# The first batch of an attention and MLP kernel, loaded with seven consecutive tokens to a partition

## The chip, the cores and the metric

The kernel runs on one core of a Trainium2 chip. The metric is the device time of one execution in microseconds, as a median of several runs. Its engines are named as in the profile: PE multiplies matrices (PEld loads its weights), DVE, ACT and POOL work on vectors, SP issues transfers. Each engine takes its instructions in order, and waits on semaphores for the others.

## The reference

`q`, `k`, `v` are (8, 12, 448, 64): 8 batches, 12 heads, 448 tokens, 64 dimensions, float32.

```python
def rmsnorm(x, g):
    rms = np.sqrt(np.mean(x * x, axis=-1, keepdims=True) + 1e-06)
    return x / rms * g
q_n, k_n = (rmsnorm(q, g_q), rmsnorm(k, g_k))
scores = np.matmul(q_n, k_n.transpose(0, 1, 3, 2)) / np.sqrt(64)
attn = softmax(scores)
x = np.matmul(attn, v)          # then heads side by side: (8, 448, 768)
xn = (x - mean(x)) / np.sqrt(var(x) + 1e-06) * g_ln
out = x + np.maximum(xn @ w_ch1, 0.0) @ w_ch2      # 768 -> 3072 -> 768
```

## The kernel before

**Tiling.** Heads go in pairs (48 of them, six to a batch). A pair has seven *groups* of 128 rows by 64 columns for each of q, k, v: for either head three groups with tokens 3p, 3p+1, 3p+2 on partition p (tokens 0 to 383, "main", `load_main`, L128), and one group with the last 64 tokens of both heads, one head on either half of the partitions ("left", `load_left`, L136). One or two pairs make a *unit*; batch 0 is units 0 to 3 (one, one, two, two pairs), later batches have three units each.

**Preparing a unit** (`pieces`, L190). The letters are those of the order below: `a`, `c` square k and q on ACT (L216); `d`, `e` sum the squares on DVE (L219); `g` takes the roots on ACT (L222, L223: logarithm, exponential), for unit 0 apart as `gq` and `gk`; `i` multiplies k by the product of the two gains, "kg" (L230, on DVE for units 0 and 1, else POOL; the product itself is L228); `j` casts that to a 16-bit high half (POOL L236, ACT L238 in unit 0) and `k` makes the low half from the difference (DVE L241); `l` scales q by its root (DVE L68); `m` duplicates it (L280, on POOL for units 1, 2 and 4); `z` casts the values to 16 bits (POOL L286, L292). The key is not scaled by its root: the exponential of the scores takes it as its scale, one number to each partition.

**Attention of a pair.** `K` (`trans_k`, L309) and `Q` (`trans_q`, L321) turn the groups over on PE into one row of PSUM, and copy that to `kU` and `qU` (DVE L319, ACT L334 or DVE L336). `S p.i` (`scores`, L340) multiplies group i of the keys with all queries of the head (L354; the left group L364, L365) and takes the exponential on ACT (L372). `V p.i` multiplies these with the values (L409, L411), which end as a tile of tokens by 128 columns of `x` (L424 to L431). `T` takes statistics for the layer norm. From unit 8 on, transfers on SP's queue turn k and q over in place of PE (L259 to L272).

**The order.** Batch 0 stands in an order written out by hand, `ORDER`: every engine has its instructions in that order. Its beginning:

```python
b0 a0 c0 L4 i0 j0 e0 k0 gq0 l0 b1 m0 a1 c1 K0 Q0 d0 G gk0 S0.0 S0.1 d1 e1 L5 i1 g1 j1 l1 k1 m1
z0 b2 a2 S0.2 d2 c2 S0.3 S0.4 K1 V0.0 e2 i2 S0.5 Q1 g2 l2 S0.6 S1.0 j2 V0.1 S1.1 S1.2 m2 b3
```

`L4`, `L5` load the units of batch 1. From batch 1 on, pieces of the attention of the next batch are dealt out between the chunks of the MLP of the one before (L653 up, L669 down).

**The first loads** (`load_first`, L138). They go into memory that the MLP uses later (`hT`, `w2`). SP begins with the main part of q of pair 0 and its two left halves, ACT with the same of k; POOL loads the two gains (L151) and the left part of k of pairs 1 to 5; all else follows on SP: k of pair 1 main, q left of pairs 1 to 5, then pair by pair.

**Stores** (`store`, L705): an x tile of 128 tokens goes out in one transfer of 128 rows, the left tokens in two of 64 rows.

Of the kernel before, what the change touches and what calls it, by code (L numbers as in the profile page):

```python
# [8 lines left out]
FP32 = mybir.dt.float32  # L9
# [7 lines left out]
ts = bass.ts  # L17

B, H, S, D = 8, 12, 448, 64
DM, FF = 768, 3072  # L20
NDC, NFF = DM // 128, FF // 128
NPAIR = H // 2
# [4 lines left out]
EXP_BIAS = -4.0  # L27
# [6 lines left out]


ORDER = """
b0 a0 c0 L4 i0 j0 e0 k0 gq0 l0 b1 m0 a1 c1 K0 Q0 d0 G gk0 S0.0 S0.1 d1 e1 L5 i1 g1 j1 l1 k1 m1
z0 b2 a2 S0.2 d2 c2 S0.3 S0.4 K1 V0.0 e2 i2 S0.5 Q1 g2 l2 S0.6 S1.0 j2 V0.1 S1.1 S1.2 m2 b3
V0.2 a3 V0.3 k2 c3 S1.3 K2 V0.4 S1.4 z2 V0.5 Q2 S1.5 V0.6 V1.0 i3 W0 d3 e3 S1.6 V1.1 V1.2 S2.0
j3 T0 V1.3 S2.1 S2.2 Q3 V1.4 S2.3 K3 S2.4 V1.5 V1.6 S2.5 g3 z3 S2.6 V2.0 S3.0 S3.1 V2.1 k3  # L40
S3.2 b4 S3.3 V2.2 l3 a4 V2.3 m3 S3.4 V2.4 K4 S3.5 Q4 V2.5 V2.6 S3.6 Q5 S4.0 V3.0 S4.1 V3.1 i4
V3.2 d4 T1 K5 V3.3 W1 c4 V3.4 V3.5 S4.2 S4.3 V3.6 S4.4 S4.5 W2 e4 V4.0 V4.1 j4 S4.6 S5.0 k4
S5.1 g4 V4.2 l4 S5.2 V4.3 V4.4 V4.5 S5.3 K6 V4.6 z4 V5.0 S5.4 m4 b5 V5.1 G2 S5.5 L6 V5.2 S5.6
# [33 lines left out]
class _Fast:  # L77
# [53 lines left out]
    def load_left(self, eng, n, t, b, h0, nh):  # L131
# [3 lines left out]
        for e in range(2):  # L135
            eng.dma_start(t[64 * e:64 * e + 64], left[e])  # L136

    def load_first(self):  # L138
        nc = self.nc
        flat = self.hT.rearrange("p f n -> p (f n)").bitcast(FP32)  # L140
        t = [flat[:, 2688 * n:2688 * n + 2688].rearrange("p (w g d) -> p w g d", w=NPAIR, d=D)
             for n in range(2)]
        flat = self.sh.w2.rearrange("p f n -> p (f n)").bitcast(FP32)
        t.append(flat[:, 128:128 + 2688].rearrange("p (w g d) -> p w g d", w=NPAIR, d=D))
        main = lambda eng, n, p: self.load_main(eng, n, t[n][:, p, 0:6], 0, 2 * p, 2)
        left = lambda eng, n, p=0, m=NPAIR: self.load_left(eng, n, t[n][:, p:p + m, 6], 0, 2 * p, 2 * m)
        for n, eng in ((0, nc.sync), (1, nc.scalar)):
            main(eng, n, 0)
            left(eng, n, 0, 1)
        for n in range(2):  # L150
            nc.gpsimd.dma_start(self.sh.gg[:, n], self.gs[n].unsqueeze(0).broadcast_to([128, D]))  # L151
        left(nc.gpsimd, 1, 1, NPAIR - 1)
        main(nc.sync, 1, 1)
        left(nc.sync, 0, 1, NPAIR - 1)
        for n, p in ((0, 1), (1, 2), (1, 3), (0, 2), (0, 3), (2, 0), (2, 1)):
            main(nc.sync, n, p)
        left(nc.sync, 2)
        for n, p in ((1, 4), (1, 5), (0, 4), (0, 5)):
            main(nc.sync, n, p)
        for p in range(2, NPAIR):  # L160
            main(nc.sync, 2, p)
        self.v_first = t[2]
        for u, (b, hs, m) in enumerate(UNITS):
            if b == 0:
                self.loads[u] = [x[:, hs // 2:hs // 2 + m].rearrange("p w g d -> p (w g) d")
                                 for x in t]

    def load_unit(self, u):
        nc = self.nc
        b, hs, m = UNITS[u]  # L170
        t = self.p_in.tile([128, 3, 14, D], FP32, tag="qkv", name="qkv")
        eng = self.nc.sync if u < 11 else self.nc.gpsimd
        for n in (1, 0, 2):
            self.load_main(nc.gpsimd if u == 10 and n == 2 else eng, n, t[:, n, 0:6 * m], b, hs, 2 * m)
            self.load_left(eng, n, t[:, n, 6 * m:7 * m], b, hs, 2 * m)
        self.loads[u] = [t[:, n] for n in range(3)]

# [12 lines left out]
    def pieces(self, u):  # L190
# [9 lines left out]
        def begin():  # L200
            c["t"] = self.loads.pop(u)
            c["ssq"] = self.p_n.tile([128, 2, 14], FP32, tag="ssq", name="ssq")[:, :, 0:g]
            c["rt"] = self.p_n.tile([128, 2, 14], FP32, tag="rt", name="rt")[:, :, 0:g]
            c["rb"] = self.p_n.tile([128, 2, 14], FP32, tag="rq", name="rr_all", bufs=6)[:, :, 0:g]
            c["r", 0], c["r", 1] = c["rb"][:, 0], c["rb"][:, 1]
            c["qn"] = self.p_n.tile([128, 14, 2, D], FP16, tag="qn", name="qn")[:, 0:g]
            c["khl"] = self.p_n.tile([128, 14, 2, D], FP16, tag="khl", name="khl")[:, 0:g]
            self.units[u] = (c["qn"], c["khl"], m, c["r", 1])

        def square(n):  # L210

# [6 lines left out]
        def total(n):  # L218
            nc.vector.tensor_reduce(out=c["ssq"][:, n], in_=c["sq", n], axis=AX.X, op=ALU.add)  # L219

        def root(n=slice(0, 2)):
            nc.scalar.activation(c["rt"][:, n], c["ssq"][:, n], AFT.Ln, bias=D * 1e-6)  # L222
            nc.scalar.activation(c["rb"][:, n], c["rt"][:, n], AFT.Exp, scale=-0.5)  # L223


        def kg():
            if u == 0:
# [53 lines left out]
                                                            in_=c["qn"][:, :, 0])  # L281

        def vmain():
            o = v16.rearrange("p s h j d -> p (s h) j d") if UNITS[u][0] else v16.rearrange(
                "p s h j d -> p s (h j) d")
            nc.gpsimd.tensor_copy(out=o[:, :, :, 0:D], in_=c["t"][2][:, 0:6 * m].rearrange(  # L286
                "p (h j) d -> p h j d", j=3) if UNITS[u][0] else self.v_first[:, p0:p1, 0:6])

        def vleft():
            for e in range(2):  # L290
                r = slice(64 * e, 64 * e + 64)
                nc.gpsimd.tensor_copy(  # L292
                    out=vl[r, :, e, 0:D],
                    in_=c["t"][2][r, 6 * m:] if UNITS[u][0] else self.v_first[r, p0:p1, 6])

        def vall():

# [3 lines left out]
            vleft()  # L301

        return dict(b=begin, a=lambda: square(1), c=lambda: square(0), d=lambda: total(1),
                    e=lambda: total(0), gq=lambda: root(0), gk=lambda: root(1), g=root, i=kg,
                    j=khi, k=klo, l=qn, m=qdup, v=vmain, w=vleft, x=dma_k, y=dma_q,
                    z=vall if u == 0 else lambda: (vmain(), vleft()))

# [1 line left out]
    def trans_k(self, p):  # L309
        nc, sh = self.nc, self.sh  # L310
        u, w = PAIR_UNIT[p]
        qn, khl = self.units[u][0:2]
        kT, ps = self.kU[PE_SET][:, 960 * (p % 2):960 * (p % 2) + 960], self.tr
        nc.tensor.matmul(ps[:, 0:256].rearrange("p (e o) -> p e o", e=2)[:, :, 0:D],
                         khl[:, self.group(p, 6)], sh.id16, is_transpose=True, start=True, stop=False)
        for i in range(6):
            nc.tensor.matmul(ps[:, 192 + 128 * i:320 + 128 * i], khl[:, self.group(p, i)], sh.id16,
                             is_transpose=True, start=False, stop=(i == 5))
        nc.vector.tensor_copy(out=kT, in_=ps[:, 0:960])  # L319

    def trans_q(self, p):  # L321
        nc, sh = self.nc, self.sh
        u, w = PAIR_UNIT[p]
        qn, khl = self.units[u][0:2]
        tr = self.ps_m.tile([128, 1024], FP16, tag="mlp", name="psQ") if p < NPAIR else self.tr
        ps = tr[:, 128:128 + 2 * S].rearrange("p (e s) -> p e s", e=2)
        qT = self.qU[PE_SET][:, p % 2].rearrange("p e s -> p (e s)")
        nc.tensor.matmul(ps[:, :, 384:S], qn[:, self.group(p, 6)], sh.id16, is_transpose=True,
                         start=True, stop=False)
        for i in range(6):  # L330
            nc.tensor.matmul(ps[:, i // 3, ts(i % 3, 128)], qn[:, self.group(p, i)], sh.id16,
                             is_transpose=True, start=False, stop=(i == 5))
        if p in ACT_Q:
            nc.scalar.copy(out=qT, in_=ps.rearrange("p e s -> p (e s)"))  # L334
        else:
            nc.vector.tensor_copy(out=qT, in_=ps.rearrange("p e s -> p (e s)"))  # L336
        kT = self.kU[PE_SET][:, 960 * (p % 2):960 * (p % 2) + 960]
        self.prs[p] = dict(q=qT, main=kT[:, 192:960], left=kT[:, 0:192])

    def scores(self, p, i):  # L340
# [25 lines left out]
        for d, x in enumerate(ps):  # L366
            if i < 6 or (p + d) % 2 == 0:
                o = c["E"][:, i]
            else:
                o = self.prs[p + d]["EL"] = self.p_e.tile([128, S], FP16, tag="EL", name="EL")  # L370
            g = self.group(p + d, i)
            nc.scalar.activation(out=o, in_=x[:, 0:S], func=AFT.Exp,  # L372
                                 scale=self.units[u][3][:, g:g + 1], bias=EXP_BIAS)

        if i == 6 and UNIT_PAIR[u] == p and u > 4:
            self.least(u)
# [328 lines left out]
    def store(self, b, t, cols, eng=None):  # L705

        nc, out = self.nc, self.out
        x = (self.xs[b][:, t] if t < 3 else self.xls[b // 2])[:, cols]
        if t < 3:
            nc.sync.dma_start(out[b, 0:384].rearrange("(p j) d -> p j d", j=3)[:, t, cols], x)  # L710
        else:
            for e in range(2):
                (eng if e else nc.sync).dma_start(out[b - 1 + e, 384:448, cols],
                                                  x[64 * e:64 * e + 64])


    def upto(self, target):
# [253 lines left out]
```

## Time and profile before

| | |
|---|---|
| Median of 3 runs | 605.36 us (604.11, 605.36, 605.42) |
| The profiled execution | 604.02 us, its span 602.5 us |
| PE busy | 575.8 us, 96% of the span |
| ACT, DVE, POOL busy | 358.5, 287.3, 184.8 us |
| First matmul | 9.40 us after the span's start |
| First exponential of scores | 12.81 us |
| First matmul of the MLP (L699) | about 53.3 us |

The span begins with the first instruction and ends with the last; the time adds what lies around it. Shares over the whole span hide that the stages differ: the attention of batch 0 (until about 55 us) has little of the MLP beside it, and there PE has gaps; after about 60 us it has next to none. A row of the timeline gives start and duration in us, the engine, the line, what is written from what, and in brackets how long the engine had been idle and what ended that. A DMA row gives the time from its issue to its landing.

### The profile page before, as it was taken

The page shows a single profiled execution, that of the slowest core. Times are in us where ns is not written, and L with a number is a line of the kernel's source. Part 1 is how long each engine was busy: PE and PEld are TensorE (multiplying, and loading weights), DVE is VectorE, ACT ScalarE, POOL GpSimd, SP SyncE. Part 2 cuts the span into 40 slices and gives each one's busy share as a digit, 9 for nine tenths or more (in the row PEclk, how much of TensorE's full clock was granted, in tenths as well). Part 3 has the DMA queues.
Part 4 walks back from the last instruction along what each step waited for, and adds up shares of the span by engine and source line. Part 5 has one row for each costly group of instructions (what it writes and reads, how often), then busy time and mean ns, then how long its engine had stood idle before and what let it go on. Part 6 is the DMA issues. An engine that isn't in the chain of part 4 may idle for free.

```text
span 602.5 us, 11487 instructions
## 1 busy us (share of the span) xinstructions
PE 575.8 (96%) x4500; PEld 340.0 (56%) x4500; DVE 287.3 (48%) x643; ACT 358.5 (60%) x673; POOL 184.8 (31%) x246
## 2 busy tenths in 40 slices
PE   2787999999999999999999999999999999999997
PEld 1555566654566666655566666654556666654465
DVE  5899567734256255724256255642355422350011
ACT  5996886358743598548755498537765287214300
POOL 2854432232642345423542245505322000000000
PEclk9999999999999999999999999999999999999999
DMA  8999999674956487947757386748543320040011
GB/s 218 280 192 208 209 223 193 107 216 83 149 128 132 92 132 156 166 122 123 126 117 135 104 125 153 180 106 153 112 70 88 93 62 1 27 106 0 2 53 54
DMA packets 130441, 75.25 MB, mean 125 GB/s; under 512 B 96656, under 2 KB 120544, under 8 KB 130384
## 3 DMA queue, kind: packets, MB, share of 16 engines
q1 hardware_dynamic: 113520, 44.72, 37.6%
q0 software_dynamic: 16192, 29.34, 23.2%
q8 instruction: 36, 0.59, 0.4%
q10 hardware_dynamic: 672, 0.43, 0.2%
q14 instruction: 21, 0.17, 0.1%
HBM read 52.36 MB, written 11.01 MB: 105 GB/s over the span
## 4 chain that ended last, share of the span: by engine, by line
PE 86%; DVE 3%; ACT 2%; DMA 1%; issue 1%; SPq 0%; DVEq 0%; ACTq 0%
PE psH L653 35%; PE psC L669 34%; PE psS L354 7%; PE oA L409 5%; PE oB L411 2%; PE psS L360 1%; DMA kU<-khl 1%; ACT E L372 1%; DVE stat L577 1%; ACT khl L216 1%; PE psU L699 0%; DVE x L426 0%; DVE ssq L219 0%; ACT hT L655 0%; DVE khl L241 0%
## 5 line engine op out<-in xcount | busy, mean ns | idle before, releaser
L653 PE MATMUL psH<-xnT,w 128*128 128x512 f16 (+1 forms) x1134 | 242.0, 353 | 0.0
L669 PE MATMUL psC<-w,hT 128*128 128x384 f16 (+1 forms) x1368 | 234.8, 324 | 0.0
L372 ACT ACTIVATE E<-psS,rr_all 128x448 f16<-128x448 f32 x312 | 193.3, 635 | 48.6 <-PE psS L354 47.7
L655 ACT ACTIVATE hT<-psH 128x512 f16<-128x512 f32 (+1 forms) x189 | 104.0, 550 | 131.1 <-PE psH L653 129.7
L669 PEld LDWEIGHTS <-hT 128*128 128x128 f16 x1368 | 127.1, 98 | 78.9 <-issue 4.3
L653 PEld LDWEIGHTS <-w 128*128 128x128 f16 x1134 | 102.3, 98 | 83.4 <-issue 2.9
L354 PE MATMUL psS<-qU,kU 128*128 128x448 f16 x288 | 101.1, 357 | 8.6 <-ACT E L372 5.7
L409 PEld LDWEIGHTS <-E 128*128 128x128 f16 x936 | 64.5, 98 | 44.5 <-issue 5.2
L230 POOL TENSOR_TENSOR qkv<-qkv,gprod 128x896 f32<-128x896 f32 x21 | 43.6, 2078 | 95.4 <-ACT khl L216 43.7
L409 PE MATMUL oA<-v,E 128*128 128x65 f16 x864 | 66.7, 194 | 0.1
L673 DVE SCALAR_TENSOR_TENSOR x<-psC,rs_all,x 128x384 f32<-128x384 f32 x48 | 29.2, 616 | 78.1 <-PE psC L669 77.7
L128 POOL DMA_DIRECT2D qkv<-in_k_dram x14 | 11.1, 793 | 136.7 <-ACT E L372 64.3
L411 PE MATMUL oB<-v,E 128*128 128x65 f16 x288 | 51.9, 194 | 0.1
L424 DVE RECIPROCAL rec_all<-oA 128x6 f32<-128x6 f32 x48 | 9.3, 194 | 88.2 <-PE oA L409 87.8
L219 DVE TENSOR_REDUCE ssq<-khl 128x14 f32<-128x896 f32 (+1 forms) x24 | 25.6, 1065 | 45.0 <-ACT khl L216 44.9
L354 PEld LDWEIGHTS <-kU 128*128 128x128 f16 x288 | 28.1, 98 | 25.7 <-issue 5.8
L219 DVE TENSOR_REDUCE ssq<-qn 128x14 f32<-128x896 f32 (+1 forms) x25 | 26.2, 1046 | 21.8 <-ACT qn L216 21.7
L68 DVE SCALAR_TENSOR_TENSOR qn<-qkv,rr_all 128x256 f16<-128x256 f32 (+1 forms) x72 | 26.4, 425 | 18.1 <-ACT rr_all L223 18.1
L411 PEld LDWEIGHTS <-E 128*128 128x128 f16 x312 | 30.2, 97 | 0.2 <-DVE xl L431 0.2
L426 DVE TENSOR_TENSOR x<-oA,rec_all 128x384 f32<-128x384 f32 x48 | 26.8, 558 | 1.5
L577 DVE BATCH_NORM_STATS2 stat<-x 128x6 f32<-128x256 f32 (+1 forms) x75 | 26.0, 404 | 0.6
L241 DVE TENSOR_TENSOR khl<-qkv,khl 128x896 f16<-128x896 f32 x21 | 22.7, 1080 | 4.0 <-DMA qkv<-in_k_dram 3.6
(111 smaller groups left out, 444.1 us busy)
## 6 DMA issues: line engine op xcount, KB each, us to landing
out_dram<-x SPq DMA_DIRECT2D x20, 384.0 KB, 2.5
qkv<-in_v_dram POOLq DMA_DIRECT2D x15, 384.0 KB, 8.1
qkv<-in_k_dram POOLq DMA_DIRECT2D x14, 384.0 KB, 3.8
qkv<-in_q_dram POOLq DMA_DIRECT2D x14, 384.0 KB, 5.2
w<-in_moe_w_ch_dram POOLq DMA_DIRECT2D x3, 1536.0 KB, 13.3
w<-in_moe_w_ch_dram POOLq DMA_DIRECT2D x2, 2304.0 KB, 25.4
qkv<-in_k_dram SPq DMA_DIRECT2D x7, 384.0 KB, 6.1
qkv<-in_q_dram SPq DMA_DIRECT2D x7, 384.0 KB, 5.6
```

Of the source, the lines that this page charges most:

```text
L219: nc.vector.tensor_reduce(out=c["ssq"][:, n], in_=c["sq", n], axis=AX.X, op=ALU.add)
L230: (nc.vector if u in DVE_KG else nc.gpsimd).tensor_tensor(out=c["t"][1], in0=c["t"][1], in1=sh.gprod.unsqueeze(1).broadcast_to([128, g, D] ...
L354: nc.tensor.matmul(ps[0][:, 0:S], c["main"][:, ts(i, 128)], c["q"][:, ts(h, S)], start=True, stop=True)
L372: nc.scalar.activation(out=o, in_=x[:, 0:S], func=AFT.Exp, scale=self.units[u][3][:, g:g + 1], bias=EXP_BIAS)
L409: nc.tensor.matmul(oA[:, t, cs], E[:, ts(t, 128)], rhs, start=(i == 0 and t == 0), stop=(i == 6 and t == 2))
L411: nc.tensor.matmul(oB[:, cs], E[:, 320:448], rhs, start=(i == 0), stop=(i == 6))
L426: nc.vector.tensor_tensor(out=x[:, :, 128 * hp:128 * hp + 128].rearrange("p t (e d) -> p t e d", e=2), in0=oA[:, :, :, 0:D], in1=rec[:, 0: ...
L577: nc.vector.bn_stats(out=self.st[b][:, t, 6 * s:6 * s + 6], in_=x[:, c0:c1])
L653: nc.tensor.matmul(ps[:, 0:N], sh.w1[:, dc, ts(f, 128)], xnT[:, dc, 0:N], start=(dc == 0), stop=(dc == NDC - 1))
L655: nc.scalar.activation(out=hT[:, f, 0:N], in_=ps[:, 0:N], func=AFT.Relu)
L669: nc.tensor.matmul(ps[:, 0:g[1]], hT[:, f, ts(t, 128)], sh.w2[:, f, cols], start=(f == 0), stop=(f == NFF - 1))
L673: nc.vector.scalar_tensor_tensor(out=x[:, cols], in0=ps[:, 0:g[1]], scalar=self.rs[:, b, t:t + 1], in1=x[:, cols], op0=ALU.mult, op1=ALU.add)
```

## The change

Batch 0 gets another order of tokens. Partition 64e + p holds seven consecutive tokens, 7p to 7p+6, of head e of a pair, so that a pair's q or k is one transfer of 128 runs of 1,792 bytes instead of one of 256 runs of 768 bytes and two of 64 runs of 256. Pairs 2 and 3, and 4 and 5, share a transfer. The values are loaded in the order in which the scores need them.

```diff
+    def rows(self, src):
+        return src.rearrange("(w e) (p j) d -> w (e p) j d", e=2, j=7).rearrange("w r j d -> r w j d")
     def load_first(self):
...
+        self.v_first = flat[:, 128:2432].rearrange("p (h t d) -> p h t d", t=3, d=D)
+        self.vl_first = flat[:, 2432:2816].rearrange("p (w d) -> p w d", d=D)
+        def pairs(eng, n, p, m=1):
+            eng.dma_start(t[n][:, p:p + m].rearrange("p w g d -> p w (g d)"), self.rows(
+                (self.q, self.k)[n][0, 2 * p:2 * p + 2 * m]).rearrange("r w j d -> r w (j d)"))
+
+        def vals(eng, p, m):
+            src = self.v[0, 2 * p:2 * p + 2 * m].rearrange("h (p j) d -> p h j d", j=7)
+            for x in range(2):
+                eng.dma_start(
+                    self.v_first[64 * x:64 * x + 64, 2 * p:2 * p + 2 * m],
+                    src[:, :, 3 * x:3 * x + 3])
+
+        pairs(nc.scalar, 1, 0)
+        pairs(nc.sync, 0, 0)
+        for n, eng in ((0, nc.scalar), (1, nc.sync)):
+            eng.dma_start(self.sh.gg[:, n], self.gs[n].unsqueeze(0).broadcast_to([128, D]))
+        pairs(nc.sync, 1, 1)
+        pairs(nc.sync, 0, 1)
+        pairs(nc.sync, 1, 2, 2)
+        pairs(nc.sync, 0, 2, 2)
+        vals(nc.sync, 0, 2)
+        nc.sync.dma_start(self.vl_first, self.rows(self.v[0])[:, :, 6])
+        pairs(nc.sync, 1, 4, 2)
+        pairs(nc.sync, 0, 4, 2)
+        vals(nc.sync, 2, 4)
```

Group i of a pair now has token 7p + i of both heads. The transposes of batch 0 put its two halves where the two heads have them: key tile t of head e holds group t on its lower half of partitions and group t + 3 on the upper one.

```diff
+        spread = ps[:, 192:960].rearrange("p (e t x o) -> p e t x o", e=2, t=3, x=2)
         for i in range(6):
-            nc.tensor.matmul(ps[:, 192 + 128 * i:320 + 128 * i], khl[:, self.group(p, i)], sh.id16,
+            o = spread[:, :, i % 3, i // 3] if p < NPAIR else ps[:, 192 + 128 * i:320 + 128 * i]
+            nc.tensor.matmul(o, khl[:, self.group(p, i)], sh.id16,
...
-            nc.tensor.matmul(ps[:, i // 3, ts(i % 3, 128)], qn[:, self.group(p, i)], sh.id16,
+            o = ps[:, :, ts(i, 64)] if p < NPAIR else ps[:, i // 3, ts(i % 3, 128)]
+            nc.tensor.matmul(o, qn[:, self.group(p, i)], sh.id16,
```

So the keys' roots, which the exponential takes by partition, have to move as well. A new piece `n`, four small copies on POOL, does that for units 0 to 3, two of the four from one half of the partitions to the other. It stands behind the root in the order: `gk0 n0 S0.0`, `g1 n1 j1`, `g2 n2 l2`, `g3 n3 z3`.

```diff
+        def spread():
+            r = c["r", 1].rearrange("p (w j) -> p w j", j=7)
+            rp = c["rp"].rearrange("p (w i) -> p w i", i=7)
+            for h in range(2):
+                for x in range(2):
+                    nc.gpsimd.tensor_copy(out=rp[64 * x:64 * x + 64, :, 3 * h:3 * h + 3],
+                                          in_=r[64 * h:64 * h + 64, :, 3 * x:3 * x + 3])
...
-                                 scale=self.units[u][3][:, g:g + 1], bias=EXP_BIAS)
+                                 scale=self.units[u][4 if i < 6 else 3][:, g:g + 1], bias=EXP_BIAS)
```

The output rows of batch 0 follow the order of the queries, in two transfers of 64 rows a tile. In unit 10 (batch 2) POOL issues the main load of q too, and not that of v alone.

```diff
+        first = out[0].rearrange("(p j) d -> j p d", j=7)[:, :, cols]
+        if t < 3 and b == 0:
+            for e in range(2):
+                nc.sync.dma_start(first[2 * t + e], x[64 * e:64 * e + 64])
...
-            self.load_main(nc.gpsimd if u == 10 and n == 2 else eng, n, t[:, n, 0:6 * m], b, hs, 2 * m)
+            self.load_main(nc.gpsimd if u == 10 and n != 1 else eng, n, t[:, n, 0:6 * m], b, hs, 2 * m)
```

## The prediction

> **What bounds the kernel now.** The table of stretches comes first. Columns: stretch, its length, then the busy time of PE, PEld, DVE, ACT, POOL with counts, granted clock, DMA share, GB/s.
>
> ```profile
> 10.00:15.00 5.00, 3.15 (x15) 1.29 (x13) 3.62 (x8) 3.66 (x9) 0.56 (x1) 1.00 1.13 312
> 15.00:20.00 5.00, 4.02 (x27) 2.71 (x27) 3.43 (x5) 4.76 (x10) 4.75 (x6) 1.00 1.09 351
> 20.00:25.00 5.00, 3.68 (x49) 2.34 (x47) 4.03 (x6) 5.00 (x9) 3.78 (x6) 1.00 0.83 239
> 25.00:45.00 20.00, 16.11 (x218) 10.91 (x217) 19.27 (x38) 18.36 (x36) 12.39 (x15) 1.00 1.06 207
> 100.00:200.00 100.00, 99.77 (x731) 56.85 (x729) 49.60 (x111) 54.70 (x98) 32.34 (x44) 1.00 0.71 135
> ```
>
> From 100 us PE is full (99.77 of 100), and the change adds no PE work there. From 25 to 45 us DVE (19.27 of 20) and ACT (18.36) are full, so whatever is late on DVE at 25 us is late at the end. Until 25 us it is latency that counts: who waits for whom. The timeline of the start shows that (start, duration, engine, line, operation, count, in brackets the idle time before and its releaser):
>
> ```profile
> 6.84 0.58 ACT L216 ACTIVATE hT<-hT 128x448 f32<-128x448 f32 x1 [2.52 <-DMA hT<-in_k_dram]
> 7.09 0.23 DVE L228 TENSOR_TENSOR gprod<-w 128x64 f32<-128x64 f32 x1 [3.91 <-DMA w<-in_g_k_dram]
> ...
> 7.45 0.63 DVE L230 TENSOR_TENSOR hT<-hT,gprod 128x448 f32<-128x448 f32 x1
> ...
> 12.27 0.21 ACT L223 ACTIVATE rr_all<-rt 128x7 f32<-128x7 f32 x1
> ...
> 12.52 0.62 DVE L230 TENSOR_TENSOR hT<-hT,gprod 128x448 f32<-128x448 f32 x1
> ...
> 12.81 0.63 ACT L372 ACTIVATE E<-psS,rr_all 128x448 f16<-128x448 f32 x1 [0.33 <-PE psS L354]
> ```
>
> ACT waits 2.52 us for a key transfer and DVE 3.91 us for the gain g_k. From 7.45 on DVE runs the chain of unit 0 almost without a gap. At 12.27 ACT makes the key's root, and 12.81 is the first exponential.
>
> Last, who shares POOL's way to memory. POOL's instructions, then DVE's, in the same stretch:
>
> ```profile
> 19.52 0.93 POOL L236 CAST khl<-hT 128x896 f16<-128x896 f32 x1
> 21.53 1.66 POOL L280 COPY qn<-qn 128x896 f16<-128x896 f16 x1 [1.08 <-DVE qn L68]
> ```
> ```profile
> 19.73 1.67 DVE L68 SCALAR_TENSOR_TENSOR qn<-hT,rr_all 128x896 f16<-128x896 f32 x1 [1.03 <-ACT rr_all L223]
> 21.32 1.08 DVE L241 TENSOR_TENSOR khl<-hT,khl 128x896 f16<-128x896 f32 x1
> ```
>
> L68 takes 1.09 us at 66.21, and 1.67 where POOL's cast began 0.21 before it. L280 takes 0.93 at 43.34, and 1.66 where L241 began first. So a DVE operation with two inputs from memory (L230, L241, L68) and a POOL operation exclude each other, and the later one waits. It holds for short ones too: two 64x128 casts, 0.29 us each elsewhere, took 2.45 us together under L241 (64.94) and L68 (66.21):
>
> ```profile
> 65.01 2.45 POOL L292 CAST vl<-qkv 64x128 f16<-64x128 f32 x2
> ```
>
> **Step 1, the loads: -2.0 us.** Before, the square at 6.84 waits for the second 16 KB remainder of the key (issued 2.18, 4.5 us to landing), the product of gains for g_k (issued by POOL at 2.71):
>
> ```profile
> hT<-in_k_dram ACTq DMA_DIRECT2D x1, 192.0 KB, 3.4
> ...
> hT<-in_q_dram SPq DMA_DIRECT2D x1, 192.0 KB, 3.1
> ...
> w<-in_g_k_dram POOLq DMA_DIRECT2D x1, 32.0 KB, 4.3
> ```
>
> After, one transfer of 224 KB per tensor is issued at 1.06 and 1.07, in place of 192 KB, which landed at 4.4 and 4.1; I take 4.6 (estimate, a sixth more bytes). The gains come second on each queue, at 1.59, where the 16 KB remainders took 3.0 and 3.7 us: they land by 4.6 to 5.3, I take 5.0 to 5.1. Gain product 5.1 to 5.35, so kg (7.45) starts at 5.45: -2.0. The ends: as slow as POOL's 4.3 us gives 5.9 and -1.1; landing at 4.5 gives -2.6. The next pair's key, third on SP at about 2.1, lands by 7.2 at the 5.1 us that the one issued at 3.10 took; its square wants it at 9.05 - 2.0 = 7.05, and ACT has 0.94 us of idle time behind it. All later times keep before's clock; the 2.0 is taken off in the sum.
>
> **Step 2, the first spread: +0.4 us.** Four copies of 64x3 on POOL behind the key's root (ends 12.48). No row has such a copy. Casts of 128, 448 and 896 columns take 0.29, 0.56 and 0.93: 0.83 ns a column, so 0.19 us for three, and POOL's instructions start about 0.05 before the one ahead ends: 0.14 each. The floor is the 0.10 of a memset of one column, the ceiling a full 0.29. The first exponential waits for two of the copies (the fourth exponential for the rest): 12.54 + 0.14 + 0.19 = 12.87, so 12.92 against 12.81, +0.1. But L230 of unit 1 starts on DVE at 12.52 and runs to 13.14. If it is first, the copies end at 13.42: +0.65. The two starts are 0.02 apart; I take +0.4, between.
>
> **Step 3, unit 1: +1.0 us.** Its four copies wait for its root (14.32), and POOL runs in order, so the key cast (13.26 to 13.82 before) waits behind them. L68 starts on DVE 0.03 after that root and POOL reacts in 0.06, so the copies wait until 14.98, end at 15.54, and the cast runs from 15.60 to 16.16. The duplicate of the query (0.56 by its columns) follows at once on POOL, ahead of DVE's low half (L241), which needs a signal first; that ends at 17.2 instead of 15.51. The transposes of pair 1 start then, not at 16.06: +1.1, and the value casts, done at 17.9, meet the first value matmuls there. Without collision the cast ends at 15.6, the transposes start at 16.4: +0.3. Behind them on PE stand V0.0, a score and the query transposes, for which ACT waits. Ends +0.3 and +1.2; +1.0, near the rows with collisions.
>
> **Step 4, unit 2: +0.9 us.** Its key cast started at 19.52, ahead of its root's end (19.70). Now it stands behind copies that wait for that root. In sequence: L68 to 20.81, copies to 21.37, cast to 22.36, duplicate to 23.25, low half to 24.2 instead of 22.40. The transposes of pair 2 are then 1.75 late. If the low half goes ahead of the duplicate: 1.0. DVE's idle 0.28 before 24.6 absorbs a part: +0.7 to +1.5. Without collision +0.1. I take +0.9, nearer to the lower collision, as ACT has two exponentials to go.
>
> **Step 5, unit 3: +0.3 us.** Its copies wait for a root at 29.60, so the value casts (28.41 to 29.83) move to 30.3 and later, onto L241 at 30.52 and L68 at 31.53. One 0.82 us cast ahead of L241 costs DVE 0.5; ends 0 and 1.1 (0.82 + 0.29).
>
> **At nothing.** POOL's four early DMA issues go, where it idled 8.62 us after them. Transposes into two runs of 64: the form exists (L314, L328), 0.29 us beside 0.31. Four more stores near 120 us, some 0.4 us of SP each, less 0.6 for unit 10's query: unit 10 lands by 130.9 and is wanted at 140.09 (L230); unit 9's transposes land at 142.5, pair 16 is scored at 157.08. That query load takes 0.78 of POOL at 112, with value casts of pairs 16 and 17 behind it. If this cover fell, 1.0 to 2 us would show.
>
> **Sum.** -2.0 + 0.4 + 1.0 + 0.9 + 0.3 = +0.6. On the profiled execution (span 602.5, time 604.02, so 1.5 outside) 604.6. The median shown, 605.36, is 1.3 above that execution, and the forecast goes by it: 606.0. All low ends -2.1, all high +3.4. About 0.2%, 1.2 us, is what a measurement of this kernel can tell from no change: the forecast is no change.
>
> **Rivals.** *Faster:* three columns are too short to collide or POOL comes first. Then -2.0 + 0.1 + 0.3 + 0.1 = -1.5, 603.9. For it: starts 0.02 to 0.03 apart. Against it: the 2.45 us for two short casts. *Slower:* one mechanism, the exclusion at every meeting, with the duplicate always ahead of the low half: -2.0 + 0.65 + 1.2 + 1.5 + 0.5 = +1.85, 607.2. It decides once unit 2's copies end later than L68 (20.81). For it: DVE reacts 0.03 after ACT. Against it: ACT's cover. *Loads not earlier:* the pair's bytes and not the small transfers set 6.84; then the gain is 1.1 and the sum +1.5, 606.9. Against it: the 192 KB landed at 4.4. *Clock:* score matmuls (L354) take 0.53 until 19.9 and 0.35 from 20.27, though the clock column says 1.00 throughout. If the switch moves with the work, as I assume, nothing changes. If it stays on a grid of its own, pair 1's two sets of transposes (14 at 0.107 against 0.057) and two scores (0.18 each) on the path change speed: 1.0 us either way, 605.0 or 607.0.
>
> The Trainium skill, page TensorE: Matmul & The Clock Gate, section Part 1: The HAM clock gate, says the second: the gate judges by a window of 3.4 us that runs free of the kernel. By that rule the sum could come out at -0.4 or +1.6. The trace agrees that there is one switch from slow to fast; it can't show the window.
>
> **Chances.** Forecast 0.40, faster 0.21, slower 0.29, loads 0.04, clock 0.06 (half each way). So faster 0.21; within 0.2% 0.40 + 0.03 = 0.43; slower 0.29 + 0.04 + 0.03 = 0.36. The range runs from just under the faster rival to just over the slower one, 603.6 to 607.6; beyond lie the outer ends. The likeliest case alone: 604.9 to 606.5.
>
> **What would show it.** kg near 5.45; the first exponential near 11.2; copies of 0.1 to 0.2 us, or near 0.6 beside L230 and L68; K1's transposes near 15.6 (16.06 - 2.0 + 0.4 + 1.1); DVE without gaps from about 25.5. Copies of 0.3 us or more everywhere, values landing after 14 us, or a gap at 140 or 157 us would prove me wrong.

## The result and the profile after

| | median | range | runs |
|---|---|---|---|
| before | 605.18 us | 604.11 to 605.42 | 6 |
| after | 610.61 us | 610.45 to 611.61 | 6 |

The changed kernel is slower: the ratio is 1.0095, 95% interval 1.0085 to 1.0106. Forecast were 606.0 us and a range of 603.6 to 607.6. The profiled execution of the kernel before (604.02 us) lies 1.2 below its median and that of the changed one (611.61 us, span 609.9) 1.0 above its own, so the two traces are 7.4 us apart where the medians are 5.4 apart.

Lines of code have moved: kg is L252 (L230 before), the low half L263 (L241), the key cast L258 (L236), the duplicate L302 (L280), the copies of piece `n` L245, the roots L236 and L237, the exponential L397 (L372), the key's transposes L336 and L341 (L314, L317).

First the table of stretches of the changed kernel, with the same columns as in the prediction:

```profile
10.00:15.00 5.00, 2.69 (x16) 1.69 (x17) 4.15 (x8) 2.76 (x8) 1.09 (x4) 1.00 1.15 254
15.00:20.00 5.00, 2.38 (x12) 1.01 (x12) 2.42 (x3) 4.38 (x9) 3.66 (x9) 1.00 1.12 240
...
25.00:45.00 20.00, 15.14 (x178) 10.89 (x178) 16.43 (x30) 16.10 (x29) 15.68 (x19) 0.83 0.80 171
100.00:200.00 100.00, 99.15 (x751) 56.94 (x750) 54.16 (x122) 60.14 (x108) 37.06 (x49) 1.00 0.74 139
```

From 25 to 45 us DVE and ACT are no longer full (16.43 and 16.10 of 20, where it was 19.27 and 18.36), POOL has more to do (15.68 for 12.39), and the granted clock is 0.83. From 100 to 200 us PE stays full (99.15 of 100). Nearly all of the time is lost before 45 us: the first exponential of pair 7 (62.42 us in the kernel before) starts 6.52 us late, and the span ends 7.4 us late. Next the start of DVE in the timeline, then that of ACT:

```profile
8.34 0.23 DVE L250 TENSOR_TENSOR gprod<-w 128x64 f32<-128x64 f32 x1 [5.16 <-DMA w<-in_g_k_dram]
8.66 0.63 DVE L252 TENSOR_TENSOR hT<-hT,gprod 128x448 f32<-128x448 f32 x1
...
13.73 0.61 DVE L252 TENSOR_TENSOR hT<-hT,gprod 128x448 f32<-128x448 f32 x1
```
```profile
4.42 0.58 ACT L230 ACTIVATE hT<-hT 128x448 f32<-128x448 f32 x1 [0.94 <-DMA hT<-in_k_dram]
...
13.48 0.21 ACT L237 ACTIVATE rr_all<-rt 128x7 f32<-128x7 f32 x1
14.66 0.63 ACT L397 ACTIVATE E<-psS,rp 128x448 f16<-128x448 f32 x1 [0.97 <-POOL rp L245]
```

The key of pair 0 is there 2.4 us earlier (its square starts at 4.42 instead of 6.84). But DVE waits 5.16 us for the gain g_k, and kg starts at 8.66 instead of 7.45. The rows of the two gain transfers, with KB and the us from issue to landing:

```profile
w<-in_g_q_dram ACTq DMA_DIRECT2D x1, 32.0 KB, 5.9
w<-in_g_k_dram SPq DMA_DIRECT2D x1, 32.0 KB, 6.7
```

The first exponential then waits 0.97 us for POOL's copies. POOL and DVE behind that:

```profile
13.75 1.34 POOL L245 COPY rp<-rr_all 64x3 f32<-64x3 f32 x4 [12.12 <-ACT rr_all L237]
16.22 1.33 POOL L245 COPY rp<-rr_all 64x3 f32<-64x3 f32 x4 [1.14 <-DMA hT<-in_q_dram]
17.62 0.56 POOL L258 CAST khl<-hT 128x448 f16<-128x448 f32 x1
18.11 0.56 POOL L302 COPY qn<-qn 128x448 f16<-128x448 f16 x1
...
22.86 1.82 POOL L245 COPY rp<-rr_all 64x6 f32<-64x6 f32 x4 [0.28 <-PE psS L379]
24.75 0.93 POOL L258 CAST khl<-hT 128x896 f16<-128x896 f32 x1
25.62 0.93 POOL L302 COPY qn<-qn 128x896 f16<-128x896 f16 x1
```
```profile
16.20 0.63 DVE L68 SCALAR_TENSOR_TENSOR qn<-hT,rr_all 128x448 f16<-128x448 f32 x1 [1.85 <-ACT rr_all L237]
18.21 0.94 DVE L263 TENSOR_TENSOR khl<-hT,khl 128x448 f16<-128x448 f32 x1 [1.38 <-POOL khl L258]
...
22.83 1.09 DVE L68 SCALAR_TENSOR_TENSOR qn<-hT,rr_all 128x896 f16<-128x896 f32 x1 [1.01 <-ACT rr_all L237]
25.71 1.78 DVE L263 TENSOR_TENSOR khl<-hT,khl 128x896 f16<-128x896 f32 x1 [1.79 <-POOL khl L258]
```

Four copies of 64x3 take 1.33 us from the first start to the last end where DVE began L252 or L68 0.02 us before the first of them; without such a neighbour they take 0.88 (in e5, below). In units 1 and 2 the key cast stands behind them, and DVE's low half waits 1.38 and 1.79 us for the cast, and is itself slowed by the duplicate that started ahead of it (1.78 instead of 1.08). At the end of that chain PE stands idle for 2.76 us, and its matmuls are slow afterwards:

```profile
27.55 0.29 PE L336 MATMUL tr<-id,khl 128*128 128x128 f16 x1 [2.76 <-DVE khl L263]
27.63 0.84 PE L341 MATMUL tr<-id,khl 128*128 128x128 f16 x6
...
28.51 0.56 PE L379 MATMUL psS<-qU,kU 128*128 128x448 f16 x1
```

In the kernel before the six transposes of pair 2 took 0.50 and the score matmul 0.35, as the clock was up:

```profile
22.46 0.23 PE L314 MATMUL tr<-id,khl 128*128 128x128 f16 x1 [0.76 <-DVE khl L241]
22.52 0.50 PE L317 MATMUL tr<-id,khl 128*128 128x128 f16 x6
...
22.98 0.35 PE L354 MATMUL psS<-qU,kU 128*128 128x448 f16 x1
```

### The profile page after: what moved, and what is told of

It is laid out like the page before. It is cut to its first block, busy times and chain, and to the rows that moved or that the text cites. A ratio compares the mean times of both kernels' runs of the same rounds, so it can differ in the third digit from the quotient of the medians.

```text
span 609.9 us, 11481 instructions
## 1 busy us (share of the span) xinstructions
PE 577.6 (95%) x4500; PEld 341.7 (56%) x4500; DVE 288.2 (47%) x643; ACT 358.6 (59%) x673; POOL 191.2 (31%) x259
## 4 chain that ended last, share of the span: by engine, by line
PE 82%; DVE 4%; DMA 3%; ACT 2%; issue 1%; SPq 0%; DVEq 0%; ACTq 0%
PE psC L694 34%; PE psH L678 33%; PE psS L379 7%; PE oA L434 4%; DMA kU<-khl 2%; PE oB L436 1%; PE psS L385 1%; DMA qkv<-in_k_dram 1%; ACT E L397 1%; DVE stat L602 1%; ACT khl L230 1%; DVE khl L263 1%; ACT khl L260 0%; PE psU L724 0%; DVE x L451 0%
## 5 line engine op out<-in xcount | busy, mean ns | idle before, releaser
L397 ACT ACTIVATE E<-psS,rr_all 128x448 f16<-128x448 f32 x276 | 173.0, 636 | 47.4 <-PE psS L379 46.6
L252 POOL TENSOR_TENSOR qkv<-qkv,gprod 128x896 f32<-128x896 f32 x21 | 43.7, 2079 | 93.1 <-ACT khl L230 44.2
L233 DVE TENSOR_REDUCE ssq<-khl 128x14 f32<-128x896 f32 (+1 forms) x24 | 25.5, 1064 | 45.6 <-ACT khl L230 45.5
L68 DVE SCALAR_TENSOR_TENSOR qn<-qkv,rr_all 128x256 f16<-128x256 f32 (+1 forms) x72 | 26.4, 425 | 18.1 <-ACT rr_all L237 18.1
L263 DVE TENSOR_TENSOR khl<-qkv,khl 128x896 f16<-128x896 f32 x21 | 22.7, 1079 | 4.0 <-ACT khl L260 3.9
```

Source lines behind the costliest of these rows:

```text
L252: (nc.vector if u in DVE_KG else nc.gpsimd).tensor_tensor(out=c["t"][1], in0=c["t"][1], in1=sh.gprod.unsqueeze(1).broadcast_to([128, g, D] ...
L263: nc.vector.tensor_tensor(out=c["khl"][:, :, 1], in0=c["t"][1], in1=c["khl"][:, :, 0], op=ALU.subtract)
L397: nc.scalar.activation(out=o, in_=x[:, 0:S], func=AFT.Exp, scale=self.units[u][4 if i < 6 else 3][:, g:g + 1], bias=EXP_BIAS)
```

## The experiments

**The theory** was that two things cost: (T1) the gains come 1.2 us later than before where they were to come 2.0 earlier, and the copies on POOL cost some 4 us more. Rivals: the layout itself, the transfers or the stores cost it (T2); and for the gains, that they stand behind 224 KB on their queues (Q), or that 128 reads of one 256-byte row are slow by themselves (H).

All results in one table. The third column is the excess of the ratio times 605 us. The last five are how much later than in the kernel before five exponentials of the scores start on ACT in the profiled execution: group 0 and group 5 of pair 0 (before: 12.81 and 17.66 us), group 4 of pair 1 (23.91), the first of pair 2 (25.71) and of pair 7 (62.42). As before's profiled execution lies under its median, these run up to 1.5 us above what the ratios say.

| run | ratio, 95% interval | us | p0.0 | p0.5 | p1.4 | p2.0 | p7.0 |
|---|---|---|---|---|---|---|---|
| after | 1.0095, 1.0085 to 1.0106 | +5.7 | +1.85 | +3.10 | +5.20 | +6.94 | +6.52 |
| e1_no_spread | 1.0016, 1.0007 to 1.0025 | +1.0 | +1.14 | +1.14 | +1.32 | +1.32 | +1.32 |
| e2_gains_pool | 1.0131, 1.0115 to 1.0146 | +7.9 | +3.63 | +4.90 | +7.01 | +8.12 | +8.47 |
| e3_gains_rows | 1.0045, 1.0031 to 1.0059 | +2.7 | -1.47 | -0.22 | +1.88 | +3.20 | +2.83 |
| e4_spread_alone | 1.0080, 1.0067 to 1.0094 | +4.8 | +0.83 | +2.09 | +4.18 | +6.00 | +5.57 |
| e5_pool_late | 1.0058, 1.0045 to 1.0070 | +3.5 | +1.91 | +2.73 | +2.95 | +3.35 | +3.53 |
| e6_dve_spread | 1.0032, 1.0020 to 1.0045 | +1.9 | +1.33 | +1.33 | +1.82 | +2.71 | +2.69 |
| e7_dummies | 1.0089, 1.0075 to 1.0104 | +5.4 | +1.89 | +3.14 | +4.60 | +4.75 | +5.70 |
| e8_before_rows | 0.9976, 0.9967 to 0.9985 | -1.5 | -1.24 | -1.24 | -1.24 | -1.23 | -1.24 |
| e9_both_mended | 0.9981, 0.9970 to 0.9993 | -1.1 | -1.23 | -1.22 | -1.10 | +0.37 | -0.07 |
| e10_before_pe_gains | 0.9981, 0.9971 to 0.9992 | -1.1 | -0.59 | -0.59 | -0.59 | -0.59 | -0.58 |
| e11_loads_alone | 0.9991, 0.9968 to 1.0015 | -0.5 | -2.09 | -2.10 | -1.93 | -1.03 | -0.03 |
| e12_mended_dummies | 0.9962, 0.9949 to 0.9976 | -2.3 | -1.09 | -1.09 | -1.09 | -1.09 | -0.76 |
| e13_loads_dummies | 0.9954, 0.9938 to 0.9969 | -2.8 | -2.03 | -2.02 | -1.85 | -1.84 | -1.84 |

One thing has to be known for the columns p1.4 and p2.0. The clock column says 1.00 also ahead of the first switch to the full rate, so only the score matmuls show when that switch came. They go from 0.53 us or more to 0.35 between 19.37 and 20.27 us in the kernel before, between 21.64 and 22.46 in the changed one, but between 27.56 and 28.43 in e3, between 31.64 and 33.34 in e2, and in e5 here:

```profile
26.26 0.56 PE L379 MATMUL psS<-qU,kU 128*128 128x448 f16 x1
...
27.41 0.35 PE L379 MATMUL psS<-qU,kU 128*128 128x448 f16 x1
```

So e2, e3 and e5 had pair 2's keys turned over at the slow rate. What they lose from p1.4 to p2.0 (1.1, 1.3 and 0.4 us) goes with that and not with gains or copies alone; no run tested it.

**e1: the copies taken out.** In the order, `n0` to `n3` go, and:

```diff
-                                 scale=self.units[u][4 if i < 6 else 3][:, g:g + 1], bias=EXP_BIAS)
+                                 scale=self.units[u][3][:, g:g + 1], bias=EXP_BIAS)
```

> The changed kernel without the four copies on POOL; the exponentials of batch 0 take the key's roots where they lie, so they scale the keys of batch 0 by the roots of other tokens (this part of the computation is changed; the number and shape of all other instructions is the same). Theory T1 (two causes: the gains land 1.2 us later than before, and the copies hold POOL until the root and cost about 4 us behind it): the late gains stay, the copies' part goes: the first exponential near 14.0, K1's transposes near 17.3 (16.06 + 1.2) and the time near 606.5, about 4 us under the changed kernel. Rival T2 (the other layout itself costs it: the transposes into runs of 64, the later transfers, the stores): K1 stays near 19.2 and the time above 609.5.

Measured 605.65 us (the kernel before, beside it: 604.88). K2's transposes start at 23.60, K1's at 17.20, both 1.14 after those of the kernel before:

```profile
17.20 0.31 PE L336 MATMUL tr<-id,khl 128*128 128x128 f16 x1
23.60 0.23 PE L336 MATMUL tr<-id,khl 128*128 128x128 f16 x1 [0.58 <-DVE khl L263]
```

T2 falls: with the new layout, its transposes, stores and transfers, what is left is the 1.2 us of the late gains.

**e4: the copies put into the kernel before**, in the changed kernel's places:

> The kernel before with the four copies on POOL alone, in the changed kernel's places in the order; the exponentials of batch 0 take the moved roots although the keys haven't moved (so they scale the keys of batch 0 by roots of other tokens). Theory T1: 3.5 to 4.5 us slower than before, 609 to 609.7, with K1's transposes 1.9 us later than in the kernel before (near 18.0) and K2's 3.9 later (near 26.4). Rival T2 (the layout or the transfers cost it, the copies little): within 1 us of before, 606.3 at most. My prediction's own figures for the copies gave +2.6.

609.71 us, +4.8: what e1 leaves between itself and the changed kernel (0.0079 times 605 = 4.8). The copies cost that with or without the new layout, so T1 holds for them.

**e2 and e3: the gains.** e2 lets POOL issue them, as before; e3 leaves them where they are and reads other addresses:

```diff
-            eng.dma_start(self.sh.gg[:, n], self.gs[n].unsqueeze(0).broadcast_to([128, D]))
+            eng.dma_start(self.sh.gg[:, n], (self.q, self.k)[n][0, 0, 0:128])
```

> The changed kernel with the two gain transfers issued by POOL, as before. Theory Q (the gains are late because they stand behind 224 KB of keys or queries on the same queue): the gain product near 7.1 as before, or earlier, and the time 1.2 us under the changed kernel, near 609.4. Rival H (128 reads of one 256-byte row of memory are slow whoever issues them): POOL issues them later than ACT and SP do, the product stays at 7.1 at the earliest and may be at 8.3 or later; time within 1 us of the changed kernel. The two differ in what the next run does, more than in this one.

> The changed kernel with its two gain transfers reading 128 different rows (of q and k, first head) in place of one row 128 times: as many packets of the same size on the same queues at the same place, other data in place of the gains, so the keys are multiplied by something else. Rival H (one row read 128 times is what is slow): they land near 5.0 instead of 7.4 and 8.2, kg starts near 5.5, and the time falls by about 3 us, to 607.5. Theory Q (the place behind the big transfers): they land at 7.4 to 8.2 again and the time stays within 0.6 us of the changed kernel.

e2 is slower still, 612.61 us: the gain transfers take 5.5 and 7.3 us, and the product starts at 10.12. Q fails. H had the time within 1 us of the changed kernel; it is 2.0 over, with a product 1.8 us later. e3 takes 607.63, 3.0 under the changed kernel, and this is its start on DVE:

```profile
5.02 0.23 DVE L250 TENSOR_TENSOR gprod<-w 128x64 f32<-128x64 f32 x1 [1.83 <-DMA w<-in_k_dram]
5.34 0.63 DVE L252 TENSOR_TENSOR hT<-hT,gprod 128x448 f32<-128x448 f32 x1
```

The same number of packets of the same size, on the same queues at the same time, are there 3.3 us earlier when they don't all read one row. The row itself isn't slow to reach: read once each, in e10 below, the gains take 3.2 and 2.7 us. The page of the transfers shows it too: what the 16 DMA engines moved, in GB/s, in the first 14 us cut into 40 slices of 0.35 us; first the changed kernel, then e3.

```profile
GB/s 0 0 0 0 0 5 123 41 246 404 395 160 21 15 14 18 45 86 124 178 201 323 391 394 405 410 401 390 380 263 194 205 203 262 239 189 177 230 244 268
```
```profile
GB/s 0 0 0 0 0 10 77 77 338 379 381 348 391 297 143 189 338 369 317 353 348 384 377 351 257 164 218 200 187 173 162 217 269 348 403 394 385 377 355 226
```

In the changed kernel the rate falls to 14 to 21 GB/s from 4.2 to 5.6 us, although the transfers of the next pairs have been issued: what stands behind the gains waits too. The next key transfer on SP's queue, 224 KB, takes 6.8 us to land, and 3.2 in e3, where there is no such hole.

**e8: did the kernel before suffer from this as well?** Its page has the same hole, if less deep (46 to 71 GB/s at the same place):

```profile
GB/s 0 0 0 0 0 0 114 116 263 354 302 144 46 71 64 59 108 141 280 283 310 214 225 255 281 307 349 358 353 373 362 362 363 361 315 233 189 208 235 290
```

e8 is the kernel before with its gain transfers, on POOL, reading 128 different rows.

> The kernel before, with its two gain transfers (on POOL, at the same place) reading 128 different rows of q and k in place of one row 128 times, so the keys are multiplied by something else. Theory H (reading one row 128 times slows the transfer and those beside it, in the kernel before as well): the product of the gains starts at 6.2 or earlier in place of 7.09, the second remainder of the key lands before 6.8, and the time is 0.6 to 1.2 us under before, near 604. Rival (POOL's gain transfers were not slowed, only those on the two other queues are): the product stays at 7.0 to 7.1 and the time within 0.3 us of before.

603.71 us, -1.5, and in its timeline of ACT and of DVE:

```profile
5.60 0.58 ACT L216 ACTIVATE hT<-hT 128x448 f32<-128x448 f32 x1 [1.29 <-DMA hT<-in_k_dram]
```
```profile
5.80 0.23 DVE L228 TENSOR_TENSOR gprod<-w 128x64 f32<-128x64 f32 x1 [2.61 <-DMA w<-in_k_dram]
```

So the square at 6.84, which the prediction put down to the small second remainder of the key, was late because of the gains beside it. These 1.2 us hang on the gain transfers alone and need no new layout. But e8's gains are other numbers; of the kernel that keeps them (e10), the trace shows 0.6 us.

**e5 and e6: why do the copies cost so much?** e5 puts the copies of units 1 to 3 behind the work that they held up; e6 puts units 0 to 2 on DVE. The orders:

```diff
-gk0 n0 S0.0 S0.1 d1 e1 L5 i1 g1 n1 j1 l1 k1 m1 ... g2 n2 l2 ... m2 b3 ... g3 n3 z3
+gk0 n0 S0.0 S0.1 d1 e1 L5 i1 g1 j1 l1 k1 m1 n1 ... g2 l2 ... m2 n2 b3 ... g3 z3 n3
```
```diff
+gk0 d1 e1 n0 S0.0 S0.1 L5 i1 g1 j1 ... V0.0 e2 n1 i2 ... g2 l2 ... k2 n2 c3 ... g3 z3 n3
-                    nc.gpsimd.tensor_copy(out=rp[64 * x:64 * x + 64, :, 3 * h:3 * h + 3],
+                    (nc.vector if u < 3 else nc.gpsimd).tensor_copy(out=rp[64 * x:64 * x + 64, :, 3 * h:3 * h + 3],
```

> The changed kernel with the copies of units 1, 2 and 3 still on POOL, but behind the work that stood behind them: unit 1's and unit 2's behind the duplicate of their query, unit 3's behind its value casts. Unit 0's stay. Theory W (what costs is that POOL, which runs in order, waits at the copies for the root and for DVE, with the key cast, the duplicate and DVE's low half behind it): only unit 0's 0.64 us is left, K1's transposes near 17.9 (17.20 without copies + 0.7), K2's near 24.3 (23.60 + 0.7), and the time 606.0 to 606.5, some 4.3 under the changed kernel. Rival P (the copies cost by themselves, by holding POOL and DVE's way to memory wherever they stand): at least half of the 5.0 us stays, 608 or more.

> The changed kernel with the copies of units 0, 1 and 2 on DVE: unit 0's behind the sums of unit 1, where the root is 0.1 us old; unit 1's behind unit 1's second half of preparations, where DVE was idle for 1.0 us; unit 2's behind its low half, where DVE was idle for 0.7; unit 3's on POOL behind its value casts. Theory W: four copies at some 0.1 us each stand in the way at unit 0 alone, where the first exponential goes to about 14.2 (13.95 without copies); the time is 605.7 to 606.2, at or under the run with the late copies on POOL. Rival P gives 606.5 or more, since DVE is full from 25 us on.

Theory W's times were missed in both runs, and rival P's bounds (608 or more, 606.5 or more) held. e5 gives 608.72: K1's transposes start at 17.97 as W had it, but half of the cost is still there. POOL's timeline says why:

```profile
16.95 0.89 POOL L302 COPY qn<-qn 128x448 f16<-128x448 f16 x1 [1.18 <-DVE qn L68]
17.78 0.88 POOL L245 COPY rp<-rr_all 64x3 f32<-64x3 f32 x4
18.73 0.83 POOL L307 CAST v<-w 128x768 f16<-128x768 f32 x1
19.50 0.64 POOL L314 CAST vl<-w 64x128 f16<-64x128 f32 x2
20.22 2.08 POOL L252 TENSOR_TENSOR hT<-hT,gprod 128x896 f32<-128x896 f32 x1
```

POOL works without a gap there. Copies behind the duplicate push the value casts, for which PE waits 0.69 us at V0.0, ahead of Q1's transposes, and kg of unit 2. So waiting in line was about half of the price. The other half goes with POOL's own 0.9 us a unit and, in this run, with a clock that came up only at about 27 us; no run parts the two. e6 gives 607.11; now DVE's timeline, then POOL's:

```profile
13.71 0.71 DVE L245 COPY rp<-rr_all 64x3 f32<-64x3 f32 x4
...
19.95 2.04 DVE L245 COPY rp<-rr_all 64x3 f32<-64x3 f32 x4
...
24.04 2.10 DVE L245 COPY rp<-rr_all 64x6 f32<-64x6 f32 x4
```
```profile
18.72 2.08 POOL L252 TENSOR_TENSOR hT<-hT,gprod 128x896 f32<-128x896 f32 x1
20.86 0.93 POOL L258 CAST khl<-hT 128x896 f16<-128x896 f32 x1
23.25 1.66 POOL L302 COPY qn<-qn 128x896 f16<-128x896 f16 x1 [1.46 <-DVE qn L68]
```

Four copies take 0.71 us on DVE where POOL is idle, and 2.0 to 2.1 beside POOL's work: the first waits for L252's end, the third for L258's. Unit 2's stood ahead of the copy of K2 (L343), which they made late; that place was badly chosen. PE stood idle for 1.15 us ahead of K2 here too, and the granted clock is 0.50 from 23.7 to 27.1 us; that is in the 1.9 as well.

**e7: the clock.** Fourteen matmuls without use (`H14`, 384 columns each) fill PE's idle time ahead of K2:

```diff
-S1.3 K2 V0.4
+S1.3 H14 K2 V0.4
```

> The changed kernel with 14 matmuls of 384 columns more on PE, which work on no result, in the gap of 2.76 us ahead of K2's transposes (2.2 us of it at the faster rate). Theory C (PE falls back to half its rate because it is idle there, and that costs a part of what the copies cost beyond unit 2's 4.1 us): the granted clock stays 1.00 from 20 to 40 us, K2's seven transposes take 0.50 in place of 0.85, and the time falls by 0.5 to 1.0 us, to 609.6 to 610.1. Rival: ACT and DVE set the pace there and PE's rate is worth nothing: within 0.3 us of the changed kernel's 610.6; or the dummies make K2 late and it is slower.

Once up, at about 23.6 us, the clock stays at 1.00 until 54.3 us, and pair 2 starts 2.19 us earlier than in the changed kernel (+4.75 instead of +6.94). But 0.95 of that is given back by pair 4: the value casts behind unit 3's copies now meet DVE's low half, which takes 1.72 (POOL's timeline, then DVE's):

```profile
34.43 0.90 POOL L245 COPY rp<-rr_all 64x6 f32<-64x6 f32 x4 [1.36 <-ACT rr_all L237]
35.39 0.83 POOL L307 CAST v<-w 128x768 f16<-128x768 f32 x1
```
```profile
35.44 1.72 DVE L263 TENSOR_TENSOR khl<-hT,khl 128x896 f16<-128x896 f32 x1
```

In time it is 610.02 against 610.61, and the intervals of the two ratios overlap: that the clock cost something is shown by the trace, its price in this kernel isn't.

**e9 to e11: both costs mended, the gains alone mended, and the loads alone.** Each gain is read once, into one partition, and a matmul with a row of ones spreads it:

```diff
-            eng.dma_start(self.sh.gg[:, n], self.gs[n].unsqueeze(0).broadcast_to([128, D]))
+            eng.dma_start(self.sh.gg[0:1, n], self.gs[n].unsqueeze(0))
...
+        nc.tensor.matmul(self.gps[:, 0:2 * D], self.sh.row,
+                         self.sh.gg[0:1].rearrange("p n d -> p (n d)"), start=True, stop=True)
```

> The changed kernel with both costs mended. Each gain is read once, 256 bytes into one partition, and a matmul with a row of ones spreads it over the partitions; the copies of units 0 and 1 are on DVE (unit 0's behind the sums of unit 1, unit 1's behind the second sum of unit 2), those of units 2 and 3 on POOL behind the value casts of their unit. By theory H, kg starts near 5.9 (5.34 with 128 different rows, and some 0.5 for the matmul and a copy out of PSUM), 2.7 us ahead of the changed kernel; by theory W with what the late copies showed (POOL is full from 15 to 30 us, so copies cost what they push back), the copies are left with 0.6 to 1.1 us of their 5. Together 603.8 to 604.4, about 1 us under before. If it is over 605.5, one of the two theories has the size wrong.

> The kernel before with the gains read once each and spread by the matmul, nothing else changed. Theory H: as with 128 different rows, but some 0.3 to 0.5 us less of a gain, for the matmul and the copy: kg at 6.5 to 6.8 in place of 7.45, the time 0.6 to 1.3 us under before. If it comes out with the run that has both costs mended, the new order of tokens is worth nothing by itself. Rival: the gain transfer hinders no other, and the matmul's way costs what the transfer saved: within 0.3 us of before.

> The changed kernel without the four copies and with the gains from 128 different rows: the loads, transposes and stores of the change with neither of its two costs (the gains are other numbers, and the scales of the keys of batch 0 are those of other tokens). My prediction's first step gave -2.0 against before for this. If the two costs simply add, it is the run without copies, 605.65, less the 3.0 us that different rows gave: 602.6, which is 2.3 to 2.6 under before. If it is over 604, something else of the layout costs, for which late copies and gains were the cover.

e9 603.91 and e10 603.63 us, ratio 0.9981 both: with the gains read once, the old layout without copies does as well as the new one with its copies. e11 misses, 603.70 with times from 602.09 to 610.05. Its trace was 2.1 us ahead and lost 1.06 between groups 3 and 6 of pair 1, and e9 lost 1.6 there, in the stretch where the granted clock falls. e11 lost another 1.0 later, between the last exponential of pair 6 (1.04 ahead) and the first of pair 7 (0.03 ahead). There ACT waits for the key transfer of a later unit, for which neither the kernel before nor e13 waits:

```profile
59.95 0.95 ACT L230 ACTIVATE khl<-qkv 128x896 f32<-128x896 f32 x1 [1.24 <-DMA qkv<-in_k_dram]
```

For the clock, each of e9, e11 and their two successors has a line here for 20 to 25 us, in the order e9, e12, e11, e13.

```profile
20.00:25.00 5.00, 3.86 (x41) 2.80 (x38) 3.30 (x7) 4.06 (x7) 4.01 (x9) 0.70 0.97 225
```
```profile
20.00:25.00 5.00, 4.50 (x63) 3.10 (x61) 4.09 (x8) 4.91 (x9) 3.88 (x9) 1.00 0.80 218
```
```profile
20.00:25.00 5.00, 4.41 (x48) 3.53 (x49) 2.93 (x8) 4.03 (x7) 3.67 (x5) 0.66 0.72 195
```
```profile
20.00:25.00 5.00, 4.31 (x59) 3.06 (x57) 3.75 (x8) 4.91 (x9) 4.86 (x6) 1.00 0.84 232
```

**e12 and e13** are e9 and e11 with five such matmuls (`H5`) ahead of K2.

> The kernel with both costs mended, and 5 matmuls of 384 columns, which work on no result, in PE's idle time of 1.14 us ahead of K2's transposes. In its profile that kernel was 1.22 us ahead of before until the fourth exponential of pair 1 and 0.37 behind from pair 2 on, with the granted clock at 0.83 from 20 to 30 us. Theory C (the clock falls because PE is idle there): the clock stays 1.00, the lead of 1.2 us stays, and the time falls by 0.5 to 1.3 us, to 602.6 to 603.4. Rival (ACT or DVE, or the transfers, cost it): within 0.4 us of 603.9.

> The loads of the change alone (no copies, gains from 128 different rows, so gains and scales of the keys are wrong numbers), and 5 matmuls of 384 columns without use in PE's idle time of 0.83 us ahead of K2's transposes. Theory C: the 1.06 us that were lost at half the clock stay won, so batch 0 runs 2.1 us ahead of before, and the median is 602.2 to 603.0 with a smaller spread than 602.1 to 610. Rival (the clock falls anyhow, or what was lost there is lost later at the next transfer): 603.5 or more.

The clock stays up (1.00 for 0.70, 1.00 for 0.66), ACT has 4.91 us to do in place of 4.06 and 4.03, and the ratios go from 0.9981 to 0.9962 and from 0.9991 to 0.9954. The kernel before was at 605.94 beside these two and at 604.96 beside e9 and e11, so the medians fall by less (603.91 to 603.79, 603.70 to 602.74). The intervals of e9 and e12 overlap (0.9970 to 0.9976), and e13 differs from e11 by the late transfer as well. So the traces show what the fall of the clock costs, 1.6 us in e9 and 1.1 in e11 until pair 2; how much of that the time keeps is not shown. e12 leaves nothing of the reference out and has the lowest ratio of those that don't, 0.4% under the kernel before; its interval overlaps with that of e10, which has the old layout.

## Why the prediction was wrong

**Step 1 (-2.0) failed, and by the largest error.** The prediction gave the gains 3.5 us to landing because 16 KB remainders had taken 3.0 and 3.7 at that place. They took 5.9 and 6.7. What set the time is neither bytes nor place but that all 128 packets read one row (e2, e3). With other rows they land at 4.76 and 4.92 and kg starts at 5.34 (forecast 5.45), so the step was right for all but that. Instead of -2.0 it gave +1.0 (e1). The row that could have told it stood in the page of before: the rate of the transfers falls to 46 GB/s while much is in flight. The rival "Loads not earlier" reckoned with a gain of 1.1; none had the gains later than before.

**Steps 2 to 5 (+2.6) were right in their mechanism and too small: +4.8** (e4; after against e1).

- Step 2, +0.4: it became +0.71. L252 was first by 0.02 us, and the copies queued behind it: a little over the upper end given, 0.65.
- Step 3, +1.0: +1.25 (1.85 to 3.10), beyond its upper end of 1.2. A copy takes 0.18 (0.19 assumed), but the next starts 0.05 after its end and not 0.05 before: 0.23 apart instead of 0.14.
- Step 4, +0.9, is the second failed step. The low half ended at 27.50 where it was 22.40: 5.1 late, 2.0 more than the 3.1 it came with (the collision in sequence gave 1.75). The text halved this because "ACT has two exponentials to go". That cover wasn't there: ACT waited 1.99 us for PE. Then PE's idle time of 2.76 let its clock fall, and pair 2 lost another 1.74 (5.20 to 6.94) to matmuls of 0.56 in place of 0.35; in e7, with the clock up, it lost 0.15 there.
- Step 5, +0.3: nothing in the changed kernel, where unit 3 came late anyhow, and 0.9 in e7, where it didn't.

**At nothing** held: stores, transposes into two runs of 64, unit 10's transfers. e13, which has them all, keeps its 1.84 us from pair 1 to the end.

**The rivals.** "Slower" had the mechanism and the sign, with the loads' gain of 2.0 still in it. "Clock" looked for a switch that comes earlier or later. It did come later, by some 2 us in the changed kernel and by some 7 to 12 in e5, e3 and e2. But what cost 1.74 us in the changed kernel was a fall back behind it, while PE waited, which no case had. That the price of "1.0 us either way" is near what e11 lost (1.06) is luck.

**What stays open.** In the traces of the changed kernel, e3 and e8 to e12 there is a further step of 0.3 to 1.1 us between 100 and 150 us, when unit 8's keys are turned over by transfers; e1, e2, e4 to e7 and e13 have none. In e10 ACT waits 1.1 us for one of these transfers, 0.2 in the kernel before. No run was made on that. With this step the spans of e9, e10 and e11 end 0.1 to 0.5 us behind that of the kernel before, whose profiled execution lies 1.2 under its median; that they are faster rests on the ratios, not on the traces. Why one row read 128 times is slow isn't shown either, only that it is, and its price isn't fixed: issued by POOL, the two transfers took 3.5 and 4.3 us in the kernel before and 5.5 and 7.3 in e2.

## What to carry to other kernels

A transfer that fills 128 partitions from one row is a suspect on any early path, and its price is paid by what is queued beside it: look for a hole in the rate of transfers, and read the row once. A copy of a few columns costs its place in line and the engine's time, not only its own duration, above all on an engine that is full in that stretch. When a change leaves PE waiting for about a microsecond at the start, look at the granted clock behind that wait, and at the durations of equal matmuls, which also show when the clock first came up.

## What the runs showed of the hardware

**The clock falls for 3.4 us or twice that.** The granted clock is 0.50 from 25.5 to 32.3 in the changed kernel, 25.0 to 31.8 in e4, 23.7 to 27.1 in e6, 54.3 to 57.7 in e7, 22.0 to 25.4 in e9, and 20.0 to 23.4 in e11. The Trainium skill, page TensorE: Matmul & The Clock Gate, section Part 1: The HAM clock gate, gives a window of 3.4 us that runs free of the kernel; by that rule the trace agrees in the lengths, 3.4 and 6.8 us. That section has the clock fall after a window that is idle. Here PE was busy for 1.64 to 2.10 us of the 3.4 just ahead of each of the six falls; in e11 it was 2.03 us, with no idle time over 0.43 until then. The measurement decides. In the ten traces that kept the full rate, PE was busy for 2.10 to 3.29 us of the first 3.4 after the switch, so some 2.1 us parts the two (an estimate from these 16 stretches). That e11's times spread by 8 us, and those of e13 by 2.4, may come from windows that fall differently from one execution to the next; only one execution of each was traced.

**POOL and DVE exclude each other for DVE's plain copies too.** The prediction had it for DVE operations with two inputs. In e6 a copy of 64x3 with one input waited out POOL's L252. The Trainium skill, page SBUF — State Buffer, section SBUF: two separate sides, states the lock, held for a whole instruction by whoever comes first, for two inputs and for DVE's 2-port modes. By that the trace agrees: four copies took 0.71 us alone and 2.04 beside POOL.
